# Landmark scores cut into quarters of the keys and turned in 32x32 blocks on VectorE; the first expert's weights scaled by halves

## The chip, the cores and the metric

The program runs on one NeuronCore of a Trainium2 chip. The metric is the device time of one execution in microseconds (us). A core has five engines that run their own instruction streams in order and wait for each other through semaphores: PE (TensorE, matrix multiplications), DVE (VectorE), ACT (ScalarE), POOL (GpSimd) and SP (SyncE, which here only issues DMAs).

## The reference

An attention with 32 landmarks (a Nyström approximation) over 8 batches and 8 heads feeds a mixture of 8 experts, of which each token uses one.

```python
# q, k, v: (8, 8, 576, 64) f32; x: (4608, 512); w1: (8, 512, 1024); w2: (8, 1024, 512)
q_lm = q.reshape(B, H, 32, 18, D).mean(axis=3)
k_lm = k.reshape(B, H, 32, 18, D).mean(axis=3)
A  = softmax(scale * q @ k_lm.T)          # 576 x 32
Bm = softmax(scale * q_lm @ k_lm.T)       # 32 x 32
C  = softmax(scale * q_lm @ k.T)          # 32 x 576, the landmark scores
Z = Bm.T / (norm1(Bm) * norminf(Bm) + 1e-6)
for _ in range(6):
    Z = 2 * Z - Z @ Bm @ Z
x = heads_joined(A @ Z @ C @ v)
probs = softmax(normed(x) @ normed(expert_emb).T / tau)
e = argmax(probs)                          # one expert per token
out = probs[e] * (relu(x @ w1[e]) @ w2[e])
```

## The kernel before

Work is done by batch. For one batch, 8 heads lie as 2 groups `g` of 4 heads `j`; 4 heads times 32 landmarks fill the 128 partitions.

- `loads`, `load_values`, `weights` issue the DMAs on SP: k, q, v of a batch, and of each batch's expert four quarters of w1 and of w2. Which expert a batch uses is guessed early (`guess`, `choose`) and read by SP from the tile `gi`.
- `sums` adds each 18 neighbouring keys or queries into landmarks (`ksum`, `qsum`; POOL may add the first halves, the tile `half`).
- `inverse` and `powers` form Bm and the six steps of Z, on 32x32 tiles of PE with a DVE addition (line 1021, tile `ek`) and a copy of half the result (ACT line 1017 or DVE line 1019) between two steps. The result is `x0`.
- `values` computes the landmark scores: 16 matmuls of 64x32 weights over 288 keys into four PSUM banks. `peak` takes each group's maximum over all keys (`cm`, line 822), `shifted` the exponential of 576 columns with its sum (line 830). `turned` transposes the exponentials on PE, five 128x128 transposes per group (lines 878, 879), and copies them out of PSUM (`ct`, lines 883, 886). `weighted` multiplies them with v (40 matmuls) and scales by the sums (`cfac`), giving `u`.
- `queries` and `scored` make A and its f16 pair `ab`. `landmarks` joins `x0` and `u` into the batch's 64x32 matrices per head (`wt` on line 1072 for batch 0), and `bound` finds a power of two to scale them by (`hbw`).
- `first_scale` squares the four quarters of w1 (ACT, line 1335), sums them over all partitions with one small matmul and derives the scale `sc1`. `first_weights` multiplies `wt` with w1 (`ps<-wstage,wt`), `scaled` turns the product into an f16 pair `ww` (ACT line 1398, DVE line 1400).
- `first` multiplies `ab` with `ww` (three f16 products for each f32 one), `hidden` applies the relu (ACT line 1451, DVE line 1453), `second` multiplies with w2 (`w2c`, scaled by `second_weights`), `outputs` writes the result.
- `keep_warm` issues matmuls of ones on PE in the stretch before the first expert (lines 598, 600); their results are not used.

The order of the work is written out: every function is a generator that asks for one engine at a time, and `Weave.run` serves these requests in the order of the table `TURNS`. `CHOICES` says which engine takes work that two could do, `BANKS` which PSUM banks are used, and `WARM` before which PE request how many blocks of 128 columns of `keep_warm` stand. Each engine then runs its instructions strictly in that order. All matmuls but those of f16 stand in the trace twice per instruction, since f32 is done in two records. The trace calls all matmuls issued through the helper `mm` line 506.

## Time and profile before

| | |
|---|---|
| time, median of 3 runs | 409.18 us (408.19 to 413.73) |
| the profiled execution's own time | 409.37 us |
| its span, first to last instruction | 407.6 us |
| PE busy | 391.1 us, 96% of the span |
| DVE busy | 322.5 us, 79% |
| ACT busy | 252.1 us, 62% |
| POOL busy | 77.8 us, 19% |
| DMA | 77.70 MB, mean 191 GB/s |

The busy time of an engine is the union of its instructions' durations. The chain that ended last is 85% PE by the page. An engine whose share is high can still wait in one stage and hold up another in the next, so the stages are looked at one by one in the rows below.

### The profile page before, as it was taken

To read this page: it belongs to the slowest core of one execution; us is meant where nothing else is said; L and a number is where in the kernel's file an instruction comes from. 1 tells how busy PE (TensorE), PEld (TensorE's weight loads), DVE (VectorE), ACT (ScalarE), POOL (GpSimd) and SP (SyncE) were. 2 spreads that over 40 slices of the span, in tenths; PEclk is the share of its full clock that TensorE was granted. 3 is DMA by queue.
4 is the path that set the end of the run, shared out by engine and by line. 5 is a ranking of instruction groups with operands and counts; after the bars stand their busy time and mean duration, and the time that the engine had idled before them with its cause. 6 is when DMAs were issued, how large, how long until landed. Compare 5 with 4: busy or idle time off the path is not lost.

```text
span 407.6 us, 14639 instructions
## 1 busy us (share of the span) xinstructions
PE 391.1 (96%) x6113; PEld 249.2 (61%) x6113; DVE 322.5 (79%) x987; ACT 252.1 (62%) x556; POOL 77.8 (19%) x80
## 2 busy tenths in 40 slices
PE   5899999998999999999999999999999999999994
PEld 4676744666655674566754576457755585457644
DVE  4989888886797998868989699787897698777521
ACT  1277968676579667836777488545676668634300
POOL 5061145201132160202215152000300200100100
PEclk9999999999999999999999999999999999999999
DMA  8896876435399359353494497202395019140031
GB/s 309 342 326 260 341 262 228 154 103 206 123 381 363 113 193 379 148 204 117 147 397 171 150 307 219 74 29 64 95 350 200 11 43 371 41 172 25 18 129 60
DMA packets 23947, 77.70 MB, mean 191 GB/s; under 512 B 3008, under 2 KB 6336, under 8 KB 22080
## 3 DMA queue, kind: packets, MB, share of 16 engines
q1 hardware_dynamic: 23584, 76.49, 51.6%
q8 instruction: 50, 0.82, 0.8%
q10 hardware_dynamic: 288, 0.18, 0.2%
q14 instruction: 25, 0.20, 0.2%
HBM read 61.92 MB, written 14.75 MB: 188 GB/s over the span
## 4 chain that ended last, share of the span: by engine, by line
PE 85%; DVE 4%; DMA 4%; issue 2%; ACT 2%; POOL 0%; SPq 0%; ACTq 0%; POOLq 0%
PE ps L506 82%; DMA q_t<-qT 3%; PE ps L878 1%; DMA k_t<-kT 1%; PE ps L600 1%; ACT junk L1335 1%; DVE ae L928 1%; DVE ht L1453 1%; DVE ksum L680 0%; DVE w2c L1443 0%; DVE ab L952 0%; DVE cm L822 0%; ACT junk L1206 0%; PE ps L879 0%; POOL half L677 0%
## 5 line engine op out<-in xcount | busy, mean ns | idle before, releaser
L506 PE MATMUL ps<-w2c,ht 128*128 128x512 f16 (+2 forms) x1176 | 197.2, 341 | 0.9 <-issue 0.9
L506 PEld LDWEIGHTS <-ht 128*128 128x128 f16 (+1 forms) x1176 | 95.2, 102 | 83.4 <-issue 5.2
L506 PE MATMUL ps<-ab,ww 128*128 128x288 f16 x768 | 99.8, 286 | 1.4 <-ACT ec L830 1.1
L506 PEld LDWEIGHTS <-ww 128*128 128x128 f16 x768 | 73.5, 98 | 23.9 <-issue 3.8
L1451 ACT ACTIVATE ht<-ps 128x288 f16<-128x288 f32 x128 | 47.4, 411 | 28.6 <-PE ps L506 27.8
L1453 DVE SCALAR_TENSOR_TENSOR ht<-ps,ht 128x288 f16<-128x288 f32 x128 | 53.3, 448 | 4.4 <-ACT ht L1451 3.7
L1443 DVE SCALAR_TENSOR_TENSOR w2c<-wstage,wsc,w2c 128x1024 f16<-128x1024 f32 x32 | 41.8, 1307 | 1.1 <-ACT w2c L1441 1.0
L1206 ACT ACTIVATE junk<-ps 128x512 bf16<-128x512 f32 (+1 forms) x40 | 23.8, 596 | 30.3 <-DVE lg L1203 30.2
L1335 ACT ACTIVATE junk<-wstage 128x1024 bf16<-128x1024 f32 x32 | 33.8, 1056 | 1.7 <-DMA wstage<-w 1.2
L1545 ACT ACTIVATE yt<-ps,gfac 128x512 f32<-128x512 f32 (+1 forms) x30 | 18.4, 627 | 22.5 <-PE ps L506 19.9
L1441 ACT ACTIVATE w2c<-wstage,wsc 128x1024 f16<-128x1024 f32 x26 | 29.5, 1143 | 3.4 <-DVE wsc L1425 3.4
L1414 ACT ACTIVATE junk<-wstage 128x1024 bf16<-128x1024 f32 x25 | 26.4, 1055 | 4.8 <-DMA wstage<-w 4.5
L1224 POOL TENSOR_TENSOR nrm<-ssq,half 128x5 f32<-128x5 f32 x8 | 10.2, 1276 | 99.7 <-ACT junk L1206 99.7
L962 POOL TENSOR_TENSOR ae<-ae,am 128x576 f32<-128x576 f32 x14 | 17.2, 1232 | 55.5 <-DVE am L935 34.9
L962 POOL TENSOR_TENSOR ae<-ae,asum 128x576 f32<-128x576 f32 x11 | 13.0, 1187 | 76.3 <-DVE asum L791 33.7
L677 POOL TENSOR_TENSOR half<-q_t 128x576 f32<-128x576 f32 x13 | 18.4, 1413 | 36.6 <-DMA q_t<-qT 20.7
L1400 DVE SCALAR_TENSOR_TENSOR ww<-ps,wsc,ww 128x1024 f16<-128x1024 f32 (+1 forms) x18 | 20.6, 1158 | 3.9 <-ACT ww L1398 3.9
L677 POOL TENSOR_TENSOR half<-k_t 128x576 f32<-128x576 f32 x11 | 15.2, 1383 | 38.3 <-DMA k_t<-kT 24.8
L1398 ACT ACTIVATE ww<-ps,wsc 128x1024 f16<-128x1024 f32 (+1 forms) x18 | 17.4, 1016 | 7.8 <-DVE wsc L1348 5.0
L506 PE MATMUL ps<-ek 32*32 32x64 f32 (+1 forms) x768 | 16.2, 214 | 0.8 <-DVE ek L1021 0.6
L1203 DVE TENSOR_REDUCE lg<-ps 128x8 f32<-128x64 f32 (+1 forms) x40 | 8.8, 221 | 10.3 <-ACT junk L1206 6.4
L506 PEld LDWEIGHTS ps<-ek 32*32 32x32 f32 x768 | 11.6, 105 | 8.4 <-issue 4.0
(215 smaller groups left out, 522.6 us busy)
## 6 DMA issues: line engine op xcount, KB each, us to landing
wstage<-w SPq DMA_DIRECT2D x64, 512.0 KB, 6.3
v<-v SPq DMA_DIRECT2D x16, 512.0 KB, 5.1
k_t<-kT SPq DMA_DIRECT2D x7, 1152.0 KB, 9.7
...
```

The costliest lines, as they stand in the source:

```text
L506: pe.matmul(o, lhsT, rhs, start=start, stop=stop)
L677: pool.tensor_tensor(out=half, in0=sv[:, :, :, 0:9], in1=sv[:, :, :, 9:18], op=ALU.add)
L962: pool.tensor_tensor(out=x, in0=x, in1=z, op=op)
L1206: act.activation(junk[lo:hi, 0:512].rearrange("p (j g x) -> p j g x", j=4, g=2), pfv[lo:hi, :, n, :, 0:D], AF.Square, accum_out=ssq[lo:hi, ...
L1335: act.activation(junk, stage[1, b, q], AF.Square, accum_out=sq[:, q:q + 1])
L1400: vec.scalar_tensor_tensor(out=ww[:, 1], in0=pw, scalar=sc, in1=ww[:, 0], op0=ALU.mult, op1=ALU.subtract)
L1414: act.activation(junk, stage[2, b, q], AF.Abs, accum_out=sq[:, q:q + 1])
L1441: act.activation(w[:, 0], st, AF.Copy, scale=sc)
L1443: vec.scalar_tensor_tensor(out=w[:, 1], in0=st, scalar=sc, in1=w[:, 0], op0=ALU.mult, op1=ALU.subtract)
L1451: act.activation(ht[:, 0, r], ph[:, 0:HS], AF.Relu)
L1453: vec.scalar_tensor_tensor(out=ht[:, 1, r], in0=ph[:, 0:HS], scalar=0.0, in1=ht[:, 0, r], op0=ALU.max, op1=ALU.subtract)
L1545: act.activation(yt[:, 0:n], py[:, 0:n], AF.Copy, scale=fac)
```

## The change

The keys are cut into quarters of 144. In `values`, partition block `32*q` now holds key quarter `q`, and a head's scores lie in the columns: 32 matmuls over 144 keys replace 16 over 288. `peak` takes the maximum of each head and quarter (8 columns over both groups), and the new `joined` combines the four quarters of a head across partitions: one copy, one maximum, one scaling and four combinations, all of 8 columns. `shifted` takes the exponential in four pieces of 144 columns per group, and then DVE transposes the group's 640 columns in 32x32 blocks straight into `ct`; PE's transposes, their PSUM banks and the copies out are gone. `weighted` gets the sums over quarters by four small matmuls with a stacked identity (`ps<-cs,ident`) and multiplies quarter blocks with v, whose layout in memory follows: 160 rows per quarter, 16 of them zero, in one DMA per group instead of two.

In `first_scale` batch 0's w1 gets a scale for each half of its quarters, so that `scaled` needs two squares instead of four for the first half; `second_weights` evens out the two scales in w2, and `first` of batch 0 goes by halves of the hidden units. `rows` reduces the logits of two or three chunks in one DVE instruction. `keep_warm` uses bf16 instead of f32r. The tables `TURNS`, `CHOICES`, `BANKS` and `WARM` are new; lines of the tables are shown only as far as they begin.

```diff
+QS = S // 4
+NB = -(-QS // M)
...
 TURNS = (
-    "060606060606000033330033000707340808340c0c0100000b0b3a3a3a01010100380001393i013h010c0c383h3j3k0101380138010101"
...
+    "06060b060b0706333306060700000000333c083c01000036010001083636013f0134340c013434013g343h010c01343h0c013h3h3h3h3h"
...
-WARM = {21: 42, 51: 15, 61: 6, 77: 3, 91: 10, 107: 7, 130: 19, 142: 18, 148: 3, 158: 7, 189: 27}
+WARM = {20: 41, 38: 14, 55: 12, 77: 20, 87: 10, 101: 3, 107: 16, 115: 15, 124: 7, 135: 1, 138: 20, 151: 9, 153: 7, 211: 28}
...
-    vts = [cst.tile([P, 5, 256], F32, name=f"v{i}") for i in range(BUFS["v"])]
-    for t in vts:
-        pool.memset(t[0:64, 4], 0.0)
+    vts = [cst.tile([P, NB, 256], F32, name=f"v{i}") for i in range(BUFS["v"])]
+    ects = [cst.tile([P, S + 2 * M - QS % M - M], F32, name=f"ec{i}") for i in range(2)]
+    for t in ects:
+        pool.memset(t[:, S:], 0.0)
...
-    onesr = ones.bitcast(F32R)
-    widths = deque((512, 512, 288, 288, 256, 256, 128, 128))
     def keep_warm(n):
-        left = n * P
-        while left:
-            k = widths[0] if left >= widths[0] else left // P * P or 96
-            widths.rotate(-1)
-            left = max(left - k, 0)
-            if k % P:
-                pe.matmul(warmth[:, 0:k], onesr, bc(onesr[:, 0:96].unsqueeze(1), [P, k // 96, 96]), start=True, stop=True)
-            else:
-                pe.matmul(warmth[:, 0:k], onesr, bc(onesr.unsqueeze(1), [P, k // P, P]), start=True, stop=True)
+        for i in range(0, n, 4):
+            k = min(n - i, 4)
+            pe.matmul(warmth[:, 0:k * P], ones16, bc(ones16.unsqueeze(1), [P, k, P]), start=True, stop=True)
...
-        sp.dma_start(v_t[:, 0:4, :], v[b, gg, 0:512 * 256].rearrange("(p c x) -> p c x", p=P, c=4))
-        sp.dma_start(v_t[64:P, 4, :], v[b, gg, 512 * 256:S * 256].rearrange("(p x) -> p x", p=64))
+        sp.dma_start(v_t.rearrange("p c x -> p (c x)"), v[b, gg])
...
-        ecs = [wk.tile([P, S], F32, name="ec", bufs=BUFS["ec"]) for _ in range(2)]
-        cm = wk.tile([P, 2], F32, name="cm", bufs=3)
-        cs = wk.tile([P, 2], F32, name="cs", bufs=3)
-        neg = wk.tile([P, 2], F32, name="cneg", bufs=3)
-        work = T(515, 32, cols=1600, tiles="heads")
+        cm = wk.tile([P, 2, 2, 2], F32, name="cm", bufs=1)
+        cs = wk.tile([P, 4, 2], F32, name="cs", bufs=3)
+        work = T(515, 64, cols=1600, tiles="heads")
         pc, done = yield from take(work, QUAD, "quad")
-        pcv = pc.rearrange("p (g i) x -> p g i x", g=2)[:, :, :, 0:HS]
-        for i in range(2):
-            if i:
+        pcv = pc[:, :, 0:2 * QS].rearrange("p (g a) (c x) -> p g a c x", g=2, c=2)
+        for g in range(2):
+            if g:
                 yield work
-            for g in range(2):
-                for j in range(4):
-                    h = head(g, j)
-                    r = slice(64 * (h % 2), 64 * (h % 2) + 64)
-                    mm(pcv[32 * j:32 * j + 32, g, i], sums_of["q", b][r, h // 2], kt[b][r, h // 2, HS * i:HS * i + HS])
+            for c in range(2):
+                for q in range(4):
+                    for a in range(2):
+                        r = slice(64 * a, 64 * a + 64)
+                        mm(pcv[32 * q:32 * q + 32, g, a, c], sums_of["q", b][r, 2 * g + c], kt[b][r, 2 * g + c, QS * q:QS * q + QS])
+            wv.add(peak(b, g, pcv[:, g], cm))
+        wv.add(joined(b, pcv, cm, cs, done))
         wv.add(weighted(b, cs))
-        for g in range(2):
-            wv.add(peak(b, g, pcv[:, g], ecs[g], neg, cm, cs, done))
         wv.tally(("kuse", b), 2)
-    def peak(b, g, pc, ec, neg, cm, cs, done):
+    def peak(b, g, pc, cm):
         yield "sleep", LAT["pe"]
         yield V(S)
-        vec.tensor_reduce(cm[:, g:g + 1], pc, axis=AX.XY, op=ALU.max)
-        yield V(1)
-        vec.tensor_scalar(neg[:, g:g + 1], cm[:, g:g + 1], -SCALE / SEG, None, op0=ALU.mult)
-        wv.add(shifted(b, g, pc, ec, neg, cs, done))
-
-    def shifted(b, g, pc, ec, neg, cs, done):
-        yield "sleep", LAT["dve"]
-        yield A(S, 165)
-        act.activation(ec.rearrange("p (i x) -> p i x", i=2), pc, AF.Exp, bias=neg[:, g:g + 1], scale=SCALE / SEG,
-                       accum_out=cs[:, g:g + 1])
+        vec.tensor_reduce(cm[:, g], pc, axis=AX.X, op=ALU.max)
+        wv.tally(("cm", b), 2)
+
+    def joined(b, pc, cm, cs, done):
+
+        yield "wait", ("cm", b)
+        cm = cm.rearrange("p g a c -> p (g a c)")
+        up = wk.tile([64, 8], F32, name="cup", bufs=1)
+        lo = wk.tile([M, 8], F32, name="clo", bufs=1)
+        neg = wk.tile([P, 8], F32, name="cneg", bufs=2)
+        yield V2(8)
+        vec.tensor_copy(up, cm[64:P])
+        yield V2(8)
+        vec.tensor_tensor(out=up, in0=up, in1=cm[0:64], op=ALU.max)
+        yield V2(8)
+        vec.tensor_scalar(lo, up[M:64], -SCALE / SEG, None, op0=ALU.mult)
+        for q in range(4):
+            yield V2(8)
+            vec.scalar_tensor_tensor(out=neg[M * q:M * q + M], in0=up[0:M], scalar=-SCALE / SEG, in1=lo, op0=ALU.mult, op1=ALU.min)
+        wv.on(("ec", b), done)
+        for g in range(2):
+            wv.add(shifted(b, g, pc[:, g], neg, cs))
+
+    def shifted(b, g, pc, neg, cs):
+        yield A(S, 700)
+        for x in range(4):
+            a, c = x % 2, x // 2
+            act.activation(ects[g][:, QS * x:QS * x + QS], pc[:, a, c], AF.Exp, bias=neg[:, 4 * g + 2 * a + c:4 * g + 2 * a + c + 1],
+                           scale=SCALE / SEG, accum_out=cs[:, x ^ g, g:g + 1])
         wv.tally(("ec", b), 2)
-        if wv.count["ec", b] == 2:
-            done()
-        yield from turned(b, g, ec)
+        yield "get", "ct"
+        yield VT(4 * NB * M)
+        ct = cts[b, g] = wk.tile([P, 4, NB, M], F32, name="ct", bufs=BUFS["ct"])
+        e = ects[g]
+        vec.transpose(ct.rearrange("p j k m -> p j (k m)"), bass.AP(e.tensor, e.offset, [list(e.ap[0]), [QS, 4], [1, NB * M]]))
+        wv.put("ec")
+        wv.flag(("ct", b, g))
     def weighted(b, cs):
-        yield "wait", ("ec", b)
         fac = wk.tile([P, 2], F32, name="cfac", bufs=BUFS["land"])
-        yield V2(2)
-        vec.tensor_scalar(fac, cs, 1e-9, None, op0=ALU.add)
+        for g in range(2):
+            yield "wait", ("ct", b, g)
+            yield "wait", ("v", b, g)
+        work = T(575, 80, cols=1280, tiles="columns")
+        pu, done = yield from take(work, 1)
+        for j in range(4):
+            mm(pu[32 * j:32 * j + 32, 2 * D:2 * D + 2], ident4, cs[:, j])
+        for g in range(2):
+            if g:
+                yield work
+            for c in range(NB):
+                for j in range(4):
+                    mm(pu[32 * j:32 * j + 32, D * g:D * g + D], cts[b, g][:, j ^ g, c],
+                       vt[b, g][:, c, (j ^ g) * D:(j ^ g) * D + D], start=(c == 0), stop=(c == NB - 1))
+            wv.put("ct")
+            wv.tally(("vuse", b, g), 2 if b < EARLY else 1)
+        yield VP(2)
+        vec.tensor_scalar(fac, pu[:, 2 * D:2 * D + 2], 1e-9, None, op0=ALU.add)
         yield V(12)
         vec.reciprocal(fac, fac)
         yield "wait", ("rc", b)
         yield V2(2)
         vec.tensor_tensor(out=fac, in0=fac, in1=rcs[b], op=ALU.mult)
-        for g in range(2):
-            yield "wait", ("ct", b, g)
-            yield "wait", ("v", b, g)
-        work = T(575, 80, cols=1280, tiles="columns")
-        pu, done = yield from take(work, 1)
-        for g in range(2):
-            if g:
-                yield work
-            for c in range(5):
-                for j in range(4):
-                    mm(pu[32 * j:32 * j + 32, D * g:D * g + D], cts[b, g][:, c, 32 * j:32 * j + 32],
-                       vt[b, g][:, c, (j ^ g) * D:(j ^ g) * D + D], start=(c == 0), stop=(c == 4))
-            wv.put("ct")
-            wv.tally(("vuse", b, g), 2 if b < EARLY else 1)
...
-    def turned(b, gg, ec):
-        pt, done = yield from early(T(550, 10, cols=543 * 2.3), b)
-        for c in range(4):
-            pe.transpose(pt[:, 0, c * P:(c + 1) * P], ec[:, c * P:(c + 1) * P], ident)
-        pe.transpose(pt[:, 1, 0:P], ec[:, S - P:S], ident)
...
+        n0 = 0
+        while n0 < len(parts):
+            c, lo, hi, s0 = parts[n0]
+            n1 = n0 + 1
+            while n1 < len(parts) and parts[n1][1:3] == (lo, hi):
+                n1 += 1
+            cg = u * NCH + c
+            yield V(64 * (n1 - n0))
+            if n1 - n0 == 1:
+                vec.tensor_reduce(lg2[lo:hi, cg], pfv[lo:hi, :, n0, :, D:].rearrange("p j g e -> p e j g"), axis=AX.XY,
+                                  op=ALU.add)
+            else:
+                vec.tensor_reduce(lg2[lo:hi, cg:cg + n1 - n0], pfv[lo:hi, :, n0:n1, :, D:].rearrange("p j n g e -> p n e j g"),
+                                  axis=AX.XY, op=ALU.add)
+            n0 = n1
         for n, (c, lo, hi, s0) in enumerate(parts):
             cg = u * NCH + c
-            yield V(64)
-            vec.tensor_reduce(lg2[lo:hi, cg], pfv[lo:hi, :, n, :, D:].rearrange("p j g e -> p e j g"), axis=AX.XY,
-                              op=ALU.add)
...
-        sq1 = wst.tile([P, 1], F32, name="wsq1", bufs=3)
         sq = wst.tile([P, 4], F32, name="wsq", bufs=3)
-        for q in range(4):
-            yield "wait", ("w", 1, b, q)
-            yield A(1024, 143)
-            act.activation(junk, stage[1, b, q], AF.Square, accum_out=sq[:, q:q + 1])
-            wv.add(used(b, q))
-        yield V(4)
-        vec.tensor_reduce(sq1, sq, axis=AX.X, op=ALU.add)
-        f2, done = yield from total(sq1, 1)
-        yield from scale_by(inv1[:, b:b + 1], f2, 2.0 ** 59, True)
-        done()
+        parts = 1 if b else 2
+        n = 4 // parts
+        for h in range(parts):
+            sq1 = wst.tile([P, 1], F32, name="wsq1", bufs=3)
+            for q in range(n * h, n * h + n):
+                yield "wait", ("w", 1, b, q)
+                yield A(1024, 143)
+                act.activation(junk, stage[1, b, q], AF.Square, accum_out=sq[:, q:q + 1])
+                wv.add(used(b, q))
+            yield V(4)
+            vec.tensor_reduce(sq1, sq[:, n * h:n * h + n], axis=AX.X, op=ALU.add)
+            f2, done = yield from total(sq1, 1)
+            inv = inv1[:, b:b + 1] if b else inv1h[:, h:h + 1]
+            yield from scale_by(inv, f2, 2.0 ** 59, True)
+            done()
+            sc = wst.tile([P, 1], F32, name="wsc1", bufs=3)
+            yield "wait", ("hbw", b)
+            yield VP(1)
+            vec.tensor_scalar(sc, hbw[:, b:b + 1].bitcast(F32), 2.0 ** 58, inv, op0=ALU.mult, op1=ALU.mult)
+            yield V(20)
+            vec.reciprocal(sc, sc)
+            scs[b, h] = sc
+            wv.flag(("sc1", b, h))
         wv.flag(("inv1", b))
-        sc = wst.tile([P, 1], F32, name="wsc1", bufs=3)
-        yield "wait", ("hbw", b)
-        yield VP(1)
-        vec.tensor_scalar(sc, hbw[:, b:b + 1].bitcast(F32), 2.0 ** 58, inv1[:, b:b + 1], op0=ALU.mult, op1=ALU.mult)
-        yield V(20)
-        vec.reciprocal(sc, sc)
-        scs[b] = sc
-        wv.flag(("sc1", b))
...
-        yield "wait", ("sc1", b)
-        sc = scs[b]
+        half = 0 if b else qs[0] // 2
+        yield "wait", ("sc1", b, half)
+        sc = scs[b, half]
...
+        if b == 0:
+            yield VP(1)
+            vec.tensor_tensor(out=inv1[:, 0:1], in0=inv1h[:, 0:1], in1=inv1h[:, 1:2], op=ALU.max)
+            top = wst.tile([P, 1], F32, name="wtop", bufs=1)
+            yield V(20)
+            vec.reciprocal(top, inv1[:, 0:1])
+            sc2 = wst.tile([P, 2], F32, name="wsc2h", bufs=1)
+            yield VP(2)
...
-        for f, s in [(f, s) for f in range(8) for s in range(2)] if b else [(f, s) for s in range(2) for f in range(8)]:
+        for f, s in [(f, s) for f in range(8) for s in range(2)] if b else [(f + 4 * h, s) for h in range(2) for s in range(2) for f in range(4)]:
...
```

The new tables move work on all engines. Three places matter below.

DVE at the very start. `e` is the square of the expert embeddings, `es` its reduction after a matmul on PE, `ksum<-half` the first half of batch 0's key sums. Before:

```order
L607 TENSOR_TENSOR e_142<-con 64x64
L680 TENSOR_REDUCE ksum<-half 128x64
L612 TENSOR_REDUCE es<-ps 128x8
L680 TENSOR_REDUCE ksum<-k_t 128x64
L680 TENSOR_REDUCE qsum<-q_t 128x64 x2
```

Now:

```order
L680 TENSOR_REDUCE ksum<-half 128x64
L608 TENSOR_TENSOR e_145<-con 64x64
L613 TENSOR_REDUCE es<-ps 128x8
L680 TENSOR_REDUCE ksum<-k_t 128x64
L680 TENSOR_REDUCE qsum<-q_t 128x64 x2
```

The square has gone behind the first key sum, and its reduction, which waits for PE, still stands ahead of the other sums.

DVE between batch 0's scores and the end of its powers (`ek` line 1021 before, 1027 now, is one step of Z). Before, from the first transposed query scores on:

```order
L928 STREAM_TRANSPOSE ae<-ps 128x576
L1019 COPY ek<-ps 128x64
L1021 TENSOR_TENSOR ek<-ek,ps 128x64
L928 STREAM_TRANSPOSE ae<-ps 128x576
L935 TENSOR_REDUCE am<-ae 128x18
L1021 TENSOR_TENSOR ek<-ek,ps 128x64
L935 TENSOR_REDUCE am<-ae 128x18
L680 TENSOR_REDUCE qsum<-half 128x64
L1021 TENSOR_TENSOR ek<-ek,ps 128x64
L680 TENSOR_REDUCE ksum<-k_t 128x64
L1021 TENSOR_TENSOR ek<-ek,ps 128x64
```

Now:

```order
L854 STREAM_TRANSPOSE ct<-ec_125 128x640
L934 STREAM_TRANSPOSE ae<-ps 128x576
L771 SCALAR_TENSOR_TENSOR ek<-ps,rct,ident_80 128x32 x2
L934 STREAM_TRANSPOSE ae<-ps 128x576
L1025 COPY ek<-ps 128x64
L1027 TENSOR_TENSOR ek<-ek,ps 128x64
L941 TENSOR_REDUCE am<-ae 128x18
L1025 COPY ek<-ps 128x64
L1027 TENSOR_TENSOR ek<-ek,ps 128x64
L854 STREAM_TRANSPOSE ct<-ec_126 128x640
L680 TENSOR_REDUCE qsum<-half 128x64
L1025 COPY ek<-ps 128x64
```

Two block transposes of 640 columns and two more copies of `ek` stand among the power steps.

PE ahead of the first expert, from the last power step of batch 0 on (`ek,u` makes `wt`, `wstage,wt` is the product with w1; `ones` alone is filling). Before:

```order
L506 MATMUL ps<-ek,u 64x32 x8
L506 MATMUL ps<-ksum,qsum 32x32 x8
L600 MATMUL ps<-ones 128x256
L600 MATMUL ps<-ones 128x128
L506 MATMUL ps<-wstage,wt 32x256 x16
L600 MATMUL ps<-ones 128x128 x2
L600 MATMUL ps<-ones 128x512
L600 MATMUL ps<-ones 128x128
L506 LDWEIGHTS ones_90
L506 MATMUL ps<-ws_606,ones_90 128x1
L506 MATMUL ps<-wsqw,ones 128x1
L506 MATMUL ps<-wstage,wt 32x256 x16
```

Now:

```order
L514 MATMUL ps<-ek,u 64x32 x8
L601 LDWEIGHTS ones_90
L601 MATMUL ps<-ones_90 128x512
L601 LDWEIGHTS ones_90
L601 MATMUL ps<-ones_90 128x384
L514 MATMUL ps<-ksum,qsum 32x32 x8
L514 MATMUL ps<-wstage,wt 32x256 x8
L514 MATMUL ps<-wsqw,ones 128x1
L514 MATMUL ps<-wstage,wt 32x256 x24
L514 LDWEIGHTS ones_90
L514 MATMUL ps<-ws_662,ones_90 128x1
L514 MATMUL ps<-u,ek 32x64 x8
```

The four quarters of w1 now follow each other with one small matmul between, which is the one that batch 0's bound waits for; the sums of the first half's squares were added up earlier.

## Rows read from the trace of the kernel before

**Rows 1.** Page, part 2: busy tenths of PE in 40 equal slices

```profile
PE   5899999998999999999999999999999999999994
```

**Rows 2.** Busy us per engine in stretches (start:end, length, PE, PEld, DVE, ACT, POOL, ...)

```profile
33.48:60.00 26.52, 25.03 (x417) 15.99 (x414) 24.42 (x72) 20.99 (x48) 6.51 (x5) 1.00 0.73 273
...
200.00:250.00 50.00, 49.31 (x654) 31.08 (x652) 43.23 (x113) 36.83 (x82) 15.14 (x11) 1.00 0.71 253
...
sum 369.02, PE 364.51 PEld 228.43 DVE 297.02 ACT 236.81 POOL 65.09; mean PE 45.56 PEld 28.55 DVE 37.13 ACT 29.60 POOL 8.14
```

**Rows 3.** PE in order of time, before the first expert: start us, us, instruction

```profile
4.87 0.65 PE L506 MATMUL ps<-e,ones 64*128 64x64 f32 x2 [4.87 <-DVE e L607]
...
11.21 1.15 PE L506 MATMUL ps<-k_t,qsum 64*32 64x288 f32 x28
12.30 0.69 PE L506 MATMUL ps<-ones,v 128*128 128x1 bf16 x14
...
17.67 0.62 PE L878 MATMUL ps<-ident,ec 128*128 128x128 f32 x4
...
19.45 0.64 PE L878 MATMUL ps<-ident,ec 128*128 128x128 f32 x4
...
24.19 1.08 PE L600 MATMUL ps<-ones 128*128 128x256 f32 x6
...
28.17 1.09 PE L506 MATMUL ps<-wstage,wt 64*32 64x256 f32 x32
...
33.48 0.90 PE L506 MATMUL ps<-ab,ww 128*128 128x288 f16 x6
34.30 0.43 PE L506 MATMUL ps<-u,ek 32*32 32x64 f32 x16
```

**Rows 4.** Chain that ended last: start us, us, what; one of its transpose groups

```profile
70.70 0.44 PE ps L878 x4
71.14 0.11 PE ps L879
```

**Rows 5.** Groups by line and shape: xcount | busy us, mean ns | idle before

```profile
L506 PE MATMUL ps<-w2c,ht 128*128 128x512 f16 x744 | 169.1, 379 | 0.0
L506 PE MATMUL ps<-wgd,ab 32*128 32x72 f16 x960 | 10.8, 194 | 0.3 <-DVE wgd L1125 0.3
L506 PE MATMUL ps<-ek 32*32 32x64 f32 x640 | 14.0, 218 | 0.7 <-DVE ek L1021 0.6
L506 PE MATMUL ps<-gr,ones 128*128 128x8 f32 x16 | 2.6, 234 | 0.0
L824 DVE TENSOR_SCALAR cneg<-cm 128x1 f32<-128x1 f32 x16 | 2.2, 143 | 0.2
```

**Rows 6.** DVE in order of time, before the first expert

```profile
6.41 0.75 DVE L680 TENSOR_REDUCE ksum<-half 128x64 f32<-128x576 f32 x1 [1.68 <-POOL half L677]
7.08 0.21 DVE L612 TENSOR_REDUCE es<-ps 128x8 f32<-128x64 f32 x1
...
16.91 0.77 DVE L928 STREAM_TRANSPOSE ae<-ps 128x576 f32<-128x576 f32 x1
17.60 0.18 DVE L1019 COPY ek<-ps 128x64 f32<-128x64 f32 x1
...
20.92 0.75 DVE L680 TENSOR_REDUCE qsum<-half 128x64 f32<-128x576 f32 x1 [0.89 <-POOL half L677]
...
23.77 0.63 DVE L848 TENSOR_TENSOR cfac<-cfac,rct 128x2 f32<-128x2 f32 x1
...
26.67 0.20 DVE L1021 TENSOR_TENSOR ek<-ek,ps 128x64 f32<-128x64 f32 x1
```

**Rows 7.** ACT in order of time: batch 0's `wt` and its `ww`

```profile
27.75 0.27 ACT L1072 COPY wt<-ps 128x128 f32<-128x128 f32 x1
...
31.02 2.42 ACT L1398 ACTIVATE ww<-ps,wsc 128x512 f16<-128x512 f32 x4 [0.17 <-DVE invw L1049]
```

**Rows 8.** POOL in order of time: what ran beside DVE's `cfac`

```profile
23.07 1.31 POOL L677 TENSOR_TENSOR half<-q_t 128x576 f32<-128x576 f32 x1
```

147 lines of the change are left out of this document (74 added, 73 removed).

## The prediction

> **What bounds the kernel now.** I read the page's slices first [rows 1]: PE is at nine tenths or more from the third slice on almost without a break. Then the stretches [rows 2]: from the first expert's first matmul at 33.48 us to the last output's matmul at 402.5 us PE is busy for 364.5 of 369.0 us, so all its waits there come to 4.5 us, 1.5 of them before 60 us. So the end is set by two things: when the first expert starts, and how much PE has to do after that. Work taken from PE behind 33.48 us shortens the kernel by its own length, unless PE waits more. Ahead of 33.48 us PE partly runs filling [rows 3], and what counts is the chain of batch 0 through DVE. My sum goes against the profiled execution's own 409.37 us (span 407.6), which lies 0.2 us over the median of the runs, 409.18.
>
> **Transposes off PE.** A group of five takes 0.44 + 0.11 = 0.55 us of the chain [rows 4]. There are 16 groups; two of them, at 17.67 and 19.45 us, stand ahead of the first expert [rows 3] and are not on its path (below). The other 14 give **-7.7 us**.
>
> **The sums' matmuls.** Four of 2 columns per batch, each twice in the trace, so 8 records. The small matmuls of 32x72 take 10.8 us for 960, 0.011 us each, where they run on several tiles of the array at once; those of 8 columns that stand alone take 2.6 us for 16, 0.16 us each [rows 5]. So 0.1 and 1.3 us a batch are the bounds. The new ones run on four column tiles, so they are nearer to the former; they load 128 rows each instead of 32, so I take 0.2 and not 0.1. Seven batches lie behind the start: **+1.4** (0.7 to 9; at the upper end each would wait for the one before, as the lone ones do).
>
> **Scores in 144 columns.** Twice the records, each half as long. Now 28 records of 288 columns take 1.15 us, 0.041 each [rows 3], so with the same columns a record of 144 takes 0.021 if the columns set the pace. The small matmuls show that the array can take one every 0.011 us, the power steps' ones take 0.022 (14.0 us for 640) [rows 5]. I take **0**; the upper bound, 0.041 as now, is a rival below. The Trainium skill (TensorE: Matmul & The Clock Gate, section "Wait — 56ns, not 53.3ns?") says that starts of matmuls never come closer than about 25 ns however few the columns; by it 64 records would take 1.6 us a batch. The 960 small ones at 11 ns disagree here, where tiles of the array work side by side.
>
> **The start of the first expert.** Batch 0's path is key and query sums, six power steps on DVE and PE (the last DVE addition at 26.67 us [rows 6]), `wt` at 27.75 us, product with w1, `ww` from 31.02 us [rows 7], first matmul at 33.48 us. The halved scale shortens the wait for `ww`, the values no longer pass PE. But the power steps stand on DVE, and there the change adds:
> - The square of the embeddings goes behind the first key sum. That ends at 6.41 + 0.75 = 7.16, the square takes 0.2, its matmul 0.65 [rows 3], so `es` comes at 8.0 instead of 7.08 [rows 6], and the sums behind it are as late: +0.95.
> - Ahead of the last step DVE gets two transposes of 640 columns. The next instruction starts 0.69 us after one of 576 (16.91 to 17.60 [rows 6]), so 0.77 each: 1.55. Seven small instructions in place of two, at 0.143 [rows 5]: 0.7. Two copies of `ek` more, 0.3 with their waits, and five other small ones moved forward, by their spacing 0.5. Together 3.05, of which DVE's one pause there, 0.89 before the query sum at 20.92 [rows 6], takes up its part: +2.15.
> - The product of the guess now stands ahead of the reciprocal of the inverse. It waits for the guess's matmuls, which follow the scores on PE (12.30 us now [rows 3], some 1.1 us long) and move by 0.95: to 14.4 us, when DVE, by the steps above, would be there at 13.75: +0.65.
>
> So the last step ends 3.75 us later. Behind it, PE's order is `wt` times the first quarter of w1 (0.55 us, half of what two quarters take [rows 3]), the bound's matmul (two records of the lone kind, 0.3 [rows 5]), three quarters (1.65), another lone one and the group `u,ek` (0.6 [rows 3, 5]), 28 blocks of filling (1.6 by the pace below) and the second guess (20 at 0.69 for 14, 0.9 with its wait [rows 3]): 5.6 us, where before 5.7 lay between 27.75 and 33.48. The start moves by **+3.6 us**. Ends: 0, if the DVE additions fall into waits of the chain, and 4.5, since w1's DMAs on SP wait for `gi`, which comes some 1.2 us later by the steps above, and ACT's copies of `ek` now stand behind two squares of w1. No gain ahead of it: behind the first stretch of filling (42 blocks, now 41, which ends before the query sums) there were 115 blocks at 1.08 us for 14 [rows 3], 8.9 us, and are 162 blocks at the pace of the f16 matmuls of 512 columns (169.1 us for 744, so 0.057 per 128 [rows 5]), 9.2 us; so what PE itself has to do there is as long as before, also with 1.1 us of transposes gone. One group `u,ek` (0.4 us behind the start now [rows 3]) moves ahead of it: **-0.4**.
>
> **Waits behind the start.** DVE gets per batch 1.55 + 0.7 us more, less about 0.5 for merged logit sums; ACT gets eight short exponentials for two long ones and loses the copies. In 200 to 250 us DVE is busy 43.2 of 50 [rows 2], so there is room. Of the 1.5 us that PE waits before 60 us I let half go, since work for it has piled up by the later start: **-0.7** (ends -2 and +7).
>
> **DMA.** v grows by a ninth and needs half the issues; PE waits for no v behind the start: 0.
>
> Sum: 409.37 - 7.7 + 1.4 + 0 + 3.6 - 0.4 - 0.7 = **405.6 us**.
>
> **The rivals.**
> - *The start keeps its time.* For it: the halved scale takes two squares of about 1.1 us off the path to `ww`, and the values' path has lost PE. Against: the additions on DVE are sure, and the power steps run through it. If the start stays, 402.0 us; with the lower ends of the sums' matmuls and the waits, 400. Chance 0.25, of which 0.11 under 401.0.
> - *DVE becomes the bound between 60 and 300 us*, and the kernel gets slower. A batch takes PE some 45 us there; it loses 1 us, while DVE's 39 us (43.2 of 50 [rows 2]) become 40.7, over 92% of the 44 left. In an in-order engine as full as that, the DVE halves of `ht` and `w2c`, which PE needs, stand behind two block transposes and seven dependent small instructions. At 1 us a batch for seven batches the sum is 412.6; the kernel is slower than before once PE's waits behind the start pass 3.8 (my sum's) + 3.8 us. For it: a two-input instruction of 2 columns took 0.63 us at 23.77 [rows 6] where it needs a quarter, so small ones can be held. The Trainium skill (SBUF — State Buffer, "Who interferes with whom") says that a VectorE instruction with two SBUF inputs waits for the whole of a GpSimd instruction that reads SBUF; five of the seven new ones are such. The row agrees: it ends soon after the POOL instruction that ran from 23.07 for 1.31 us [rows 8]. Against: the 4.5 us of waits now. Chance 0.2, of which 0.03 over 417.4.
> - *The score matmuls are bound by their number.* At the 0.041 us of now 64 would take 2.6 us a batch instead of 1.3, 9 us in seven batches; half-way to the power steps' 0.022 [rows 5], at 0.031, 2.0 us, so +0.7 a batch and 4.9 in all: 410.5 us. Against: the small matmuls. Chance 0.1.
> - My forecast, 403 to 408.5 us: 0.45.
>
> **Numbers.** A change under 2% (401.0 to 417.4 us around the median) is not told from none here. Faster: 0.11 from the first rival. Slower: 0.03 from the second. The range 401.0 to 410.5 holds my case, the rest of the first rival (0.14), most of the third (0.08) and half of the second (0.1): about 0.8.
>
> **What would show it.** In the changed profile: no transposes under `ec`; the first `ab,ww` matmul near 37.1 us; `es` near 8.0 us, the last step of batch 0 near 30.4; PE waits of 3 to 5 us after the start; 64 score records in 1.2 us. It is wrong if the start stays at 33.5 us, if the score groups take over 1.5 us, or if PE waits over 8 us behind the start.

## The result, and the profile after

| | before | changed |
|---|---|---|
| median of 20 runs each, same chip | 409.86 us (408.09 to 414.31) | 413.06 us (410.78 to 415.07) |
| profiled execution, its span | 409.37, 407.6 us | 413.29, 411.6 us |
| first `ab,ww` matmul | 33.48 us | 37.91 us |
| from there to PE's last matmul | 369.0 us | 368.7 us |
| PE's idle time in that stretch | 4.5 us | 7.1 us |

The ratio of the times is 1.0074, 95% interval 1.0049 to 1.0098: no change by the 2% bound, and 7.5 us over the forecast. The start came 4.4 us later (3.6 forecast); behind it 0.3 us were gained instead of some 7. Of the changed kernel's 20 executions 12 have a mean granted clock of 0.996 or less, with a median of 413.5 us, and 8 have more, with 411.8; the profiled one is of the former.

The slices of the changed kernel, which answer to [rows 1]: behind the start PE has two slices at eight tenths and the eleventh at seven, and in that one the clock has a dent.

```profile
PE   3988899989799999999999999999999999999995
...
PEclk9999999999899999999999999999999999999999
```

The stretches from the first expert on, by engine (answering [rows 2]):

```profile
37.91:60.00 22.09, 20.34 (x298) 13.21 (x295) 20.61 (x70) 20.10 (x54) 3.31 (x3) 1.00 0.65 250
60.00:100.00 40.00, 38.61 (x820) 23.49 (x819) 36.74 (x115) 27.41 (x71) 14.99 (x12) 1.00 0.49 175
...
108.00:116.00 8.00, 5.93 (x109) 4.05 (x94) 2.77 (x14) 2.90 (x9) 0.65 (x1) 0.79 0.05 16
...
200.00:250.00 50.00, 49.68 (x697) 31.55 (x697) 45.61 (x140) 37.30 (x100) 12.92 (x10) 1.00 0.70 253
...
sum 368.69, PE 361.57 PEld 224.57 DVE 309.26 ACT 234.39 POOL 62.19; mean PE 36.16 PEld 22.46 DVE 30.93 ACT 23.44 POOL 6.22
```

PE waits early (5.9 of its 7.1 us up to 116 us) and little later. In 108 to 116 us it is idle for 2.07 us, and the mean granted clock of 0.79 means that 3.4 of the 8 us ran at 1.2 GHz instead of 2.4, some 1.7 us of work lost. What PE waited for behind the start (total us, times, longest), and its timeline at the two longest gaps:

```profile
PE ps L514 <- issue: 3.3, 2, 2.1
PE ps L514 <- DVE ht L1488: 1.5, 4, 0.8
PE ps L514 <- ACT junk L1224: 0.7, 2, 0.4
```

```profile
90.85 0.31 PE L514 MATMUL ps<-ek 32*32 32x64 f32 x6
92.40 0.60 PE L514 MATMUL ps<-ek 32*32 32x64 f32 x26 [1.25 <-issue]
...
107.75 0.53 PE L514 MATMUL ps<-wgd,ab 32*128 32x72 f16 x42 [0.32 <-ACT junk L1224]
110.35 0.66 PE L514 MATMUL ps<-wgd,ab 32*128 32x72 f16 x30 [2.06 <-issue]
```

Both gaps stand inside a group of small matmuls and have no releaser: the six before and the 26 behind the first one are one step of Z, which needs nothing new in between. In the DMA queue that carries instructions, a block of 16 KB was on its way at 90.12 to 91.01 us, up to 0.14 us before the first gap opened, and at 107.89 to 108.81 us, up to half a microsecond into the second.

In the start, `es` comes at 7.81, the last power step at 30.03 instead of 26.67 [rows 6], `wt` now from DVE (the answer to [rows 7]); then DVE waits for the second half's square, with the f16 pairs `ab` and `ww` behind it:

```profile
30.03 0.20 DVE L1027 TENSOR_TENSOR ek<-ek,ps 128x64 f32<-128x64 f32 x1
...
30.83 0.29 DVE L1078 COPY wt<-ps 128x128 f32<-128x128 f32 x1
...
35.63 0.16 DVE L1001 TENSOR_SCALAR whb<-ps 128x1 int32<-128x1 int32 x1 [1.50 <-PE ps L514]
...
36.42 0.74 DVE L958 SCALAR_TENSOR_TENSOR ab<-at,ab 128x576 f16<-128x576 f32 x1
...
37.41 0.75 DVE L1424 SCALAR_TENSOR_TENSOR ww<-ps,wsc,ww 128x512 f16<-128x512 f32 x1 [0.18 <-ACT ww L1422]
```

PE was late for that square because it stopped once more, in the product with w1 (a stop of 0.61 us at 27.17 us, ahead of the last power step, is the fourth):

```profile
32.19 1.51 PE L514 MATMUL ps<-wstage,wt 64*32 64x256 f32 x42
34.85 0.63 PE L514 MATMUL ps<-wstage,wt 64*32 64x256 f32 x6 [1.16 <-issue]
35.41 0.18 PE L514 MATMUL ps<-ws,ones 128*128 128x1 bf16 x1
```

### The profile page after: what moved, and what is told of

It reads as the page before. It is cut to its first block, busy times and chain, and to the rows that moved or that the text cites. A ratio compares the mean times of both kernels' runs of the same rounds, so it can differ in the third digit from the quotient of the medians.

```text
span 411.6 us, 15151 instructions
## 1 busy us (share of the span) xinstructions
PE 388.9 (94%) x6331; PEld 238.3 (58%) x6331; DVE 337.7 (82%) x1036; ACT 249.1 (61%) x623; POOL 74.5 (18%) x79
## 4 chain that ended last, share of the span: by engine, by line
PE 79%; DVE 11%; ACT 4%; issue 3%; DMA 2%; POOL 0%; SPq 0%; ACTq 0%
PE ps L514 77%; DVE ht L1488 2%; ACT junk L1224 1%; DMA wstage<-w 1%; PE ps L601 1%; DVE cm L820 1%; DMA k_t<-kT 1%; ACT ec L847 1%; DVE ksum L680 1%; DVE ww L1424 1%; DVE w2c L1478 1%; DVE ct L854 1%; DVE cneg L838 0%; ACT ww L1422 0%; ACT ht L1486 0%
## 5 line engine op out<-in xcount | busy, mean ns | idle before, releaser
L514 PE MATMUL ps<-ab,ww 128*128 128x288 f16 x768 | 102.0, 287 | 1.7 <-DVE ht L1488 1.5
L1486 ACT ACTIVATE ht<-ps 128x288 f16<-128x288 f32 x128 | 46.4, 419 | 48.3 <-PE ps L514 48.1
L1478 DVE SCALAR_TENSOR_TENSOR w2c<-wstage,wsc,w2c 128x1024 f16<-128x1024 f32 x28 | 35.8, 1279 | 2.4 <-ACT w2c L1476 2.3
L1357 ACT ACTIVATE junk<-wstage 128x1024 bf16<-128x1024 f32 x32 | 33.9, 1059 | 5.2 <-DMA wstage<-w 5.0
L847 ACT ACTIVATE ec<-ps,cneg 128x144 f32<-128x144 f32 x64 | 23.4, 391 | 8.8 <-DVE cneg L838 8.8
L1438 ACT ACTIVATE junk<-wstage 128x1024 bf16<-128x1024 f32 x26 | 27.4, 1053 | 0.5
L1476 ACT ACTIVATE w2c<-wstage,wsc 128x1024 f16<-128x1024 f32 x18 | 20.6, 1149 | 7.5 <-DVE wsc L1449 4.7
L968 POOL TENSOR_TENSOR ae<-ae,am 128x576 f32<-128x576 f32 x13 | 15.1, 1159 | 45.2 <-DVE am L941 22.8
L677 POOL TENSOR_TENSOR half<-k_t 128x576 f32<-128x576 f32 x11 | 14.3, 1299 | 41.6 <-DMA k_t<-kT 23.4
```

Of the source, the lines that this page charges most:

```text
L514: pe.matmul(o, lhsT, rhs, start=start, stop=stop)
L677: pool.tensor_tensor(out=half, in0=sv[:, :, :, 0:9], in1=sv[:, :, :, 9:18], op=ALU.add)
L847: act.activation(ects[g][:, QS * x:QS * x + QS], pc[:, a, c], AF.Exp, bias=neg[:, 4 * g + 2 * a + c:4 * g + 2 * a + c + 1], scale=SCALE / ...
L968: pool.tensor_tensor(out=x, in0=x, in1=z, op=op)
L1357: act.activation(junk, stage[1, b, q], AF.Square, accum_out=sq[:, q:q + 1])
L1438: act.activation(junk, stage[2, b, q], AF.Abs, accum_out=sq[:, q:q + 1])
```

## The experiments

Two explanations were set against each other. **Place:** PE stops where a new block of its instructions begins, if the work ahead of it was issued quickly, and the half clock follows such a stop; so the place of the work in PE's list costs time, not the work. (That blocks of instructions are the reason is a guess; the runs test the place.) **VectorE:** the added instructions on DVE make PE wait. In all runs the ratio is to the kernel before, run on the same chip beside it.

### Moving the changed kernel along PE's list

The first stretch of filling, ahead of batch 0's scores, is cut into more matmuls: 82 of 64 columns, 41 of 128, 21 of 256 or 55 of 96 in place of 11, so everything behind stands 71, 30, 10 or 44 matmuls later in PE's list. The first of the four:

```diff
     def keep_warm(n):
+        if n == WARM[20]:
+            for i in range(n * P // 64):
+                pe.matmul(warmth[:, 0:64], ones16, ones16[:, 0:64], start=True, stop=True)
+            return
```

> The changed kernel with its first stretch of filling (41 blocks of 128 columns, ahead of batch 0's scores) cut into 82 matmuls of 64 columns instead of 11 of up to 512: same columns, 71 more matmuls ahead of everything. Theory (PE runs out of instructions): PE's stalls without a releaser follow instruction fetches and depend on where in the list of instructions a fetch falls, so the stalls of 1.16 us at 33.69, 1.25 us at 91 and 2.06 us at 108 us come at other places and with other lengths, and where no stall of 2 us is left the half clock of 3.4 us is gone too: 409.5 to 413 us. Rival (the stalls belong to the work that stands there, a wait that the profile does not show): the three stalls stay where they are in the work, with their lengths, and the time stays at 412.5 to 413.5 us.

> As the run before, but the same stretch as 41 matmuls of 128 columns, so 30 more matmuls than the changed kernel. Theory (PE runs out of instructions): stalls at other places than in the changed kernel and than with 71 more; 409.5 to 413 us. Rival (stalls belong to the work): same stalls, 412.5 to 413.5 us.

> The changed kernel with the first filling (41 blocks) in 21 matmuls of 256 columns instead of 11: 10 more ahead. Theory (place): between the changed kernel (413.1 us) and its run with 30 more (410.0 us), with stops at records 478, 1501 and 1884 as long as the work there lets them be; 410 to 413.5 us.

> The changed kernel with the first filling in 55 matmuls of 96 columns: 44 more ahead. Theory (place): stops at the same record numbers before other work; 409.5 to 413 us. If all of the changed kernel's places give 409.5 us or more while the kernel before reaches 408 to 409.5 at most of its places, the change itself is worth nothing or less; if the two spread over the same range, the place decides.

| more matmuls ahead | median | ratio, interval | start | start to PE's end |
|---|---|---|---|---|
| 0 (changed kernel) | 413.06 | 1.0074 (1.0049 to 1.0098) | 37.91 | 368.7 |
| 10 | 413.35 | 1.0053 (1.0012 to 1.0094) | 37.59 | 371.3 |
| 30 | 410.02 | 0.9981 (0.9939 to 1.0023) | 37.99 | 365.6 |
| 44 | 409.82 | 0.9987 (0.9951 to 1.0023) | 35.85 | 368.2 |
| 71 | 410.23 | 1.0006 (0.9971 to 1.0042) | 35.83 | 368.6 |

The same work, in the same order, takes 3 us less at three places. They gain it in two ways. With 30 more, 108 to 116 us has no gap and the full clock, and behind the start 3.1 us are gained:

```profile
108.00:116.00 8.00, 8.00 (x139) 5.66 (x135) 6.43 (x23) 4.60 (x14) 2.17 (x2) 1.00 0.43 135
...
sum 365.61, PE 360.01 PEld 223.81 DVE 310.11 ACT 234.51 POOL 61.73; mean PE 120.00 PEld 74.60 DVE 103.37 ACT 78.17 POOL 20.58
```

With 44 and 71 more the stretch behind the start is as long as the changed kernel's. There the start lacks both its stops, the 0.6 us ahead of the last power step and the 1.2 us in the product with w1, and the first expert begins at 35.8 us.

The stops of over 0.15 us without a releaser, added up behind the start, account for the spread. They come to 3.3 us in the changed kernel, 4.6 with 10 more, 0.8 with 30, 3.5 with 44 and 2.7 with 71; only the first two of these have the half clock behind one, 1.7 us of work lost each. Without stops and half clock the stretch takes 363.7 to 365.9 us in all five, and 366.7 in the kernel before, which has 2.3 us of stops.

### The start

Here the order in `TURNS` is edited by the pairs of a new table `MOVES`: the turn named first is served just ahead of the other. One kernel has the embeddings' square (turns 12, 13) first again, ahead of the key sum (8). One takes the first half's `ww` ahead of the second half on ScalarE (quarter 0 before 1) and the first `ab` and `ww` ahead of the second half's square on VectorE (from turn 186 on), and drops the 28 blocks of filling ahead of the guess (the entry `211: 28` of `WARM`). Then both, and both with the first filling at two more places; one more kernel moves the guess (turns 211, 212, 218) behind the first six matmuls of the first expert, with the bank of its turn moved in `BANKS` too. Its table has all the pairs; the other kernels have the first two, the next twelve, or these fourteen.

```diff
+MOVES = [(12, 8), (13, 8), (187, 186), (188, 186), (201, 186), (192, 186), (191, 186), (195, 186), (197, 186), (198, 186), (205, 186), (216, 199), (203, 202), (219, 202), (211, 217), (212, 222), (218, 222)]
...
+    for who, ahead in MOVES:
+        item = next(x for x in seq if x[0] == who)
+        seq.remove(item)
+        seq.insert([x[0] for x in seq].index(ahead), item)
```

> The changed kernel with the square of the embeddings ahead of the first key sum on VectorE, as before the change. Theory (the start is late by what VectorE does ahead of it): es comes at 7.1 us instead of 7.81, the last power addition at 29.3 instead of 30.03, the first matmul of the first expert at 37.2 instead of 37.91, and the time falls by 0.7 us. Rival (the chain is held by w1's DMAs and by PE's stalls, not by the sums): es early, the first expert at 37.9 as now, time the same.

> The changed kernel with the first half's scaling of w1 ahead of everything of the second half on VectorE and ScalarE (ww of quarter 0 ahead of quarter 1, the second square's chain behind the first ab and ww), and without the 28 blocks of filling that stand on PE between the last product with w1 and the guess. Theory (the new wait of 1.50 us for the second half and the filling behind it hold the start): the wait of whb at 34.13 us is gone, PE goes from u,ek at 35.9 us to the guess and the first expert starts at 36.4 instead of 37.91; the time falls by 1 to 1.5 us, more or less by what the stalls do. Rival (VectorE is the bound between 36 and 56 us, so an early start only waits there): the start is 1.5 us earlier and PE waits at least 1 us longer for ht or ww before 56 us; the time falls by under 0.5 us.

> The edits of the two runs before together. Theory: the first expert starts at 35.7 us, the time is 2 us below the changed kernel's. Rival (VectorE holds the stretch behind the start): start at 35.7, time within 1 us of the changed kernel's.

> The same with the first filling as 41 matmuls of 128 columns, the run in which no stall of 2 us and no half clock were seen. If stalls and start add up: 3 us (stalls, half clock) and 2 us (start) below the changed kernel, 407.5 to 408.5 us. If the stalls fall elsewhere since PE's list has 7 matmuls fewer and other times: 409 to 411 us.

> The eighth run's kernel with the second guess on PE behind the first expert's first six matmuls, and its VectorE work behind the last ww, since it waited 1.06 us for whb. Theory (PE waits there for the place of the guess in the order): the first expert starts at 35.2 us instead of 36.50 and the time falls by 0.5 to 1 us, to 407.5 to 408.2 us. Rival (four ww of 0.74 us each on VectorE hold the stretch): start at 35.2, the wait for ww grows from 0.89 us to about 2, time as the eighth run's.

> The eighth run's edits (embeddings' square first, first half's scaling ahead of the second's, no filling ahead of the guess) with the first filling in 55 matmuls of 96 columns: 37 more matmuls ahead than the changed kernel, where the eighth run had 23. If the edits make the gain: 408 to 409 us again. If its place in the list does: 409.5 us or more.

| edit | median | ratio, interval | start |
|---|---|---|---|
| square first | 411.17 | 1.0000 (0.9963 to 1.0037) | 37.97 |
| first half first, no filling | 417.08 | 1.0142 (1.0086 to 1.0198) | 37.23 |
| both | 414.54 | 1.0075 (1.0037 to 1.0112) | 35.78 |
| both, 23 more ahead | **408.64** | 0.9929 (0.9897 to 0.9961) | 36.50 |
| both, 37 more ahead | 409.07 | 0.9968 (0.9932 to 1.0003) | 36.75 |
| both, 23 more, guess later | 409.18 | 0.9962 (0.9929 to 0.9994) | 35.60 |

With the square first `es` came at 7.09, but in that trace the last power step came at 30.10, as in the changed kernel. This doesn't show that the square is off the path: here PE started the work behind the first filling at 11.47 us, 0.7 us after "both" did (10.77), though the filling is the same (see the last section), and DVE then waited for the scores. In "both", with the same list up to there, `es` came at 7.02 and the last power step at 29.24, 0.8 us earlier than in the changed kernel. The ratio of 1.0000 lies below the changed kernel's 1.0074, and the intervals don't meet; the one trace is of the longest of its eleven executions, 416.65 us, so what the others gained isn't seen.

The second edit was to save 1 to 1.5 us and raised the ratio from 1.0074 to 1.0142, and the third left it at 1.0075 with a start 2.1 us earlier: they have 7 matmuls fewer ahead and met the longest stops yet, with two stretches of 3.4 us at the half clock in each trace. PE's timeline shows where it stopped. Of "both":

```profile
90.40 0.41 PE L515 MATMUL ps<-ek 32*32 32x64 f32 x13
93.61 0.52 PE L515 MATMUL ps<-ek 32*32 32x64 f32 x19 [2.80 <-issue]
...
108.88 0.58 PE L515 MATMUL ps<-wgd,ab 32*128 32x72 f16 x49 [0.32 <-ACT junk L1225]
111.27 0.37 PE L515 MATMUL ps<-wgd,ab 32*128 32x72 f16 x23 [1.82 <-issue]
```

The changed kernel stopped behind 6 of the 32 records of that step of Z and behind 42 of the 72 of the gating group; with 7 fewer ahead it stops behind 13 and 49. The stop stays at its number in the list, and the work moves past it. The same kernel with 30 more matmuls ahead (the fourth row) is 5.9 us faster and beats the kernel before. At the next place the gain is half as large, and its interval includes 1; its trace has the half clock from 34.6 to 41.4 us. The start of the fourth row is still 3 us behind that of before. Moving the guess brought the start to 35.60 us and gave no time: the 1.1 us that PE waited for `whb` ahead of the guess went, the one for `ww` (DVE line 1430) stayed at 1.0 us where the rival forecast 2, a new one of 0.6 us for ACT came, and the trace has 3.4 us of half clock from 39.7 us on. Which of these took the gain back is open.

### The kernel before along its own list

Its first filling of 42 blocks is cut into 42 f32r matmuls of 128 columns, 42 bf16 ones, or 11 bf16 ones of 512, in place of 18.

> The kernel before with its first filling (42 blocks) as 42 matmuls of 128 columns instead of 18, so that everything behind stands 24 matmuls later in PE's list. Theory (PE stops at fixed places of its list, about every 128 matmul records, if cheap work stands there): the stops of 0.88 us at 83.7 and 1.27 us at 99.2 us go or move, new ones appear where small matmuls have come to those places; the time may move by up to 3 us either way, 407 to 413 us. Rival (the kernel before has no such places, its stops belong to the work): stops at the same work, time within 0.5 us of the kernel before.

> The kernel before with its first filling (42 blocks) as 42 bf16 matmuls of 128 columns instead of 18 f32r ones: 24 matmuls more ahead, and a filling that is not longer, so the first expert starts at 33 to 34 us. Theory (the place in PE's list sets the stops): the stops at 1371 and 1753 stand before work that is 24 records earlier, as in the ninth run, where they took 3.0 and 1.6 us instead of 1.0 and 1.4: 410 to 413 us. Rival (the ninth run's 10 us were its late start alone): 409 to 410 us.

> The same filling in bf16 matmuls of 512 columns, 11 instead of 18: 7 matmuls fewer ahead. Theory (place): stops at the same record numbers before work that is 7 records later; 407 to 413 us, with PE's time from the first expert to the end differing from 369.0 us by what its stops of over 0.5 us differ from 2.3. Rival: as the kernel before within 0.5 us.

| | median | ratio, interval | start | start to PE's end |
|---|---|---|---|---|
| 24 more, f32r | 419.72 | 1.0162 (1.0063 to 1.0262) | 41.44 | 371.6 |
| 24 more, bf16 | 410.73 | 1.0008 (0.9972 to 1.0045) | 33.45 | 369.5 |
| 7 fewer, bf16 | 413.49 | 1.0039 (0.9994 to 1.0085) | 39.56 | 367.2 |

(Filling and transposes stand in the trace once per instruction.) The first says little on place: the 42 f32r matmuls took 9.2 us instead of 4.4, and the start came 8 us later. The second shows the stops in the kernel before too. First the row of before, then the one with 24 more ahead:

```profile
82.34 1.61 PE L506 MATMUL ps<-w2c,ht 128*64 128x256 f16 x26
84.83 1.39 PE L506 MATMUL ps<-w2c,ht 128*64 128x256 f16 x22 [0.88 <-issue]
```

```profile
80.61 0.30 PE L506 MATMUL ps<-w2c,ht 128*64 128x256 f16 x2
82.95 1.28 PE L506 MATMUL ps<-w2c,ht 128*64 128x256 f16 x20 [2.03 <-issue]
```

It stops behind 2 of these matmuls where it stopped behind 26. Still its time is that of before within 0.5%: other waits were shorter, and PE is idle for 5.1 us behind the start instead of 4.5. With 7 fewer ahead PE stopped for 1.23 us at 26.2 us, in the last power step, and from 28.9 to 39.1 us, nearly up to the first expert, it ran at the lower clock:

```profile
26.00:28.00 2.00, 0.77 (x20) 0.55 (x14) 1.56 (x3) 1.97 (x4) 1.16 (x1) 1.00 0.85 316
28.00:30.00 2.00, 2.00 (x41) 1.72 (x40) 0.64 (x2) 0.52 (x3) 0.00 (x0) 0.72 0.95 331
30.00:32.00 2.00, 2.00 (x34) 0.80 (x33) 1.60 (x9) 1.16 (x4) 1.16 (x1) 0.50 0.98 353
```

### What the transposes on PE cost

In the kernel before the ten `pe.transpose` of a batch are left out (the copies to `ct` read `ec` itself), doubled, or left out with the 42 f32r matmuls of filling.

> The kernel before with PE's transposes of the exponentials left out; the copies that took their results out of PSUM copy the untransposed exponentials instead, and the count of wrong guesses is held at zero, so the outputs are not the reference's. Theory (the transposes were on the path with their whole length, and the changed kernel lost the gain elsewhere): 14 groups of 0.55 us behind the start go, 7.7 us, and up to 1 us ahead of it: 401 to 402.5 us. Rival (PE's work was not the bound, so that the other engines take the gain back as PE gets faster): 405 to 409 us, with PE waiting 4 us or more longer than 4.5 us behind the start.

> The kernel before with every transpose of the exponentials done twice on PE, with the same result. Theory (the transposes are on the path behind the start): 14 more groups of 0.55 us, +7.7 us, up to 1 us more ahead of the start, and stops that fall elsewhere, up to 2 us either way: 415 to 419 us. Rival (PE has room for them): under 412 us.

> The kernel before without the transposes (as in the third run: copies of the untransposed exponentials, count of wrong guesses held at zero, outputs not the reference's), at another place of PE's list: 24 more matmuls ahead. Theory (the transposes are worth 6.5 to 8 us and the third run's times were spread by stops and by the clock): some of the runs at 401 to 404 us, a median under 406 us. Rival (without its transposes PE is held by others or loses the clock): a median of 408 to 409 us again.

Left out: 408.95 us, ratio 0.9942 (0.9893 to 0.9992), which is in the rival's range; runs from 402.99 us on. The profiled one took 402.99, with 362.4 us from start to PE's end, 6.7 fewer than before. Doubled: 421.49, ratio 1.0250 (1.0175 to 1.0324). Its 70 further transposes behind the start add 7.64 us from one start of a matmul to the next, and the stretch is 10.4 us longer; some 4 of these are 2.3 us more of stops and 3.4 us of half clock. The third kernel took 415.99 us; its like is the kernel before with the same 42 f32r matmuls, 419.72 us. It has 366.2 us behind the start for 371.6, with 2.3 us of the difference in stops and half clock, and the two ratios' intervals overlap. So in all three traces the transposes were on the path, in the first two with 6 to 7 us of their 7.9. That the first one's median stayed 6 us over its best run goes with the clock: the two quickest, 402.99 and 404.75 us, have a mean granted clock of 0.999 and 1.000, and seven of the other eight have 0.994 or less. Why it fell in these isn't shown, since only the profiled run has a trace.

### What VectorE's additions cost

The block transposes of batches 1 to 7 cut to 32 columns; then, with 30 more matmuls ahead, also one instruction for the seven that join the maxima.

```diff
+        if n > 1:
+            vec.transpose(ct[:, 0, 0], e[:, 0:M])
...
-        vec.tensor_copy(up, cm[64:P])
...
+        vec.tensor_scalar(neg, cm, -SCALE / SEG, None, op0=ALU.mult)
```

> The changed kernel with VectorE's block transposes of batches 1 to 7 cut from 640 to 32 columns (14 instructions of 0.8 us become 14 of some 0.1), so the outputs are not the reference's; the count of wrong guesses is held at zero. Theory (VectorE is in the way only in a few stretches): 14 x 0.7 = 9.8 us go from VectorE, PE's waits for it fall by 0.5 to 1.5 us: 411 to 412.5 us. Rival (VectorE became the bound behind the start and gave the gain back): 405 to 408 us.

> The second run's kernel (30 more matmuls ahead) with what the change adds on VectorE per batch taken away: the block transposes of batches 1 to 7 cut to 32 columns and the seven small instructions that join the maxima replaced by one, so some 2.2 us less per batch on VectorE; the outputs are not the reference's, the count of wrong guesses is held at zero. Theory (VectorE's added work is what PE waits for behind the start): PE's idle time behind the start falls from 5.6 us to under 4 and the time from 410.0 to 407 to 408.5 us. Rival (the order of the work sets the waits, whatever VectorE's load): idle 5 us or more, 409.5 to 410.5 us.

The first took 412.19 us, ratio 1.0035 (0.9995 to 1.0076): no gain of 5 us, and stops of 2.0 and 1.8 us in its trace. PE's list is the changed kernel's, so the two can be compared matmul by matmul: 500 records behind the start, at 73.5 us, both are 35.6 us on. Up to there the transposes cost PE nothing; further on the longer stops hide what they may cost. The second took **404.87 us**, ratio 0.9819 (0.9724 to 0.9913, four executions), 5.1 us less than with the additions at the same place in the list. Its last power step came at 28.25 instead of 29.69 us, the first expert at 36.0 instead of 37.99, and PE was idle for 4.3 us behind it instead of 5.6:

```profile
36.00:108.00 72.00, 69.37 (x1433) 44.10 (x1431) 63.49 (x211) 53.02 (x141) 18.29 (x14) 1.00 0.55 201
...
sum 363.20, PE 358.91 PEld 223.67 DVE 294.83 ACT 234.13 POOL 61.84; mean PE 119.64 PEld 74.56 DVE 98.28 ACT 78.04 POOL 20.61
```

Batch 0's two transposes are whole in this kernel:

```profile
17.49 0.80 DVE L858 STREAM_TRANSPOSE ctt<-ec 128x640 f32<-128x640 f32 x1
...
21.22 0.83 DVE L858 STREAM_TRANSPOSE ctt<-ec 128x640 f32<-128x640 f32 x1
...
24.85 0.21 DVE L1031 TENSOR_TENSOR ek<-ek,ps 128x64 f32<-128x64 f32 x1
...
28.25 0.21 DVE L1031 TENSOR_TENSOR ek<-ek,ps 128x64 f32<-128x64 f32 x1
```

So the small instructions, six fewer, are what brought the fourth power step to 24.85 us instead of 25.83. The rest of the 2.0 us by which the start is earlier is mostly shorter stops: one of 0.25 us ahead of the last power step, for which DVE waited 0.38, is missing, and the one in the product with w1 took 1.04 us instead of 1.59. DVE does 15 us less behind the start, and PE is through that stretch 2.4 us sooner. Matmul by matmul the gain comes bit by bit: 0.6 us up to 57 us, 1.9 more between 92 and 144 us, and 0.5 between 196 and 217 us; a longer stop at 278 us (1.23 us for 0.79) takes some back. So VectorE's additions are on the path, the small ones by 1 us at the start, and both together by 2.4 behind it. How much of the latter is the small instructions and how much the transposes is open: the two runs differ in both edits and in the place.

## Why the prediction was wrong

- **Transposes, scores, sums: right.** From each matmul's start to the next, behind the first expert's start, the transposes are gone with 7.92 us (7.7 forecast), 448 records of 144 columns take 7.90 us for 224 of 288 that took 7.97 (0 forecast), the sums' matmuls 0.59 (1.4, lower end 0.7), `u,ek` 0.49 less (0.4) without the stop of 1.27 us that stood in it before. These come to some 7.9 us less. Leaving out the transposes and doubling them showed that most of their length counts.
- **"Waits behind the start" is the step that failed.** I let PE's waits fall by 0.7 us, to 3.8. They rose to 7.1 us, and PE's busy time fell by 2.9 us only. The groups of matmuls that the change left alone took 5.0 us more from start to start, gaps left out: 1.7 us are the half clock of 110 to 113.4 us. The other 3.3 us are, as I read it, waits that the union of durations hides: an `ab,ww` matmul is recorded with 0.29 us and the next starts 0.13 us later, so a wait of up to 0.16 us reads as busy. No row shows what they waited for.
- *What stood in place of that step.* First, stops of PE at fixed places of its list, with the half clock behind one: 3 us, shown by moving the same work by 30 matmuls (368.7 to 365.6 us behind the start, 413.06 to 410.02 in all). Such gaps of "issue" were 2.3 us of the 4.5 in the profile of before; the prediction has no term for them and counts them as waits that stay or go with the work. Second, VectorE: 2.4 us behind the start, shown by taking its additions away. The rival "DVE becomes the bound" had this mechanism and priced it at 1 us a batch; it is a third of that, spread from the start to 217 us. The sentence "so there is room", read from the 43.2 of 50 us in 200 to 250, missed it: 0.5 us of the gain fell between 196 and 217 us. The two come to 5.5 us of the 7.1 by which the stretch exceeded the forecast (368.7 us for 361.6); the rest is open.
- **Start: the direction and most of the size were right,** 4.43 us against 3.6, the last step 30.03 against 30.4. But that is in part luck. Of the 4.43 us, 1.8 are two stops of PE, for which the prediction had no term: at places where they are missing the start is 35.8 us, 2.4 later than before. The parts that were forecast, 3.6 us, came to less. The square cost some 0.8 us ("both" against the changed kernel; 0.95 forecast). Six small instructions fewer brought 1.0 us, where 0.7 had been forecast for five more. The wait for the guess's matmuls was 0.15 us at 13.81 us on DVE, for 0.65. What the two transposes cost there no run shows. DVE's wait of 1.50 us for the second half's square comes from the second of these stops; it is gone with 44 and 71 more matmuls ahead, where 5.3 us lie between `wt` and the first `ab,ww` matmul, for 5.6 forecast.
- **The other rivals fell as forecast:** the start did not keep its time, and the scores were not bound by their number.
- The sum, were both costs gone: with light VectorE and 30 more matmuls ahead the kernel takes 404.9 us, near the forecast of 405.6, but without work that the forecast had included. At the good places the change is worth nothing (410 us). With the start's order edited as well it was tried at three places, with ratios of 1.0075, 0.9968 and 0.9929; the best, a gain of 0.7% (0.4 to 1.0), was picked from the three.
